# Weight tiles formed as pairs of 1024 columns in the first row, x turned tile by tile, and four smaller reorderings

## The chip, the cores and the metric

The kernel runs on one core of a Trainium2 chip. The metric is device time in microseconds (us), from the start of the program to its end; the median of three runs is given. One further execution was taken with the hardware profiler. The engines are PE (TensorE: matrix products, which end in PSUM), ACT (ScalarE), DVE (VectorE), POOL (GpSimd) and SP (which here only issues DMA transfers). Each has its own instruction stream; they wait for one another by semaphores.

## The reference

```python
# x 8x8x512x64 (B, H, S, D), state 8x8x32x64 (B, H, Ns, D)
scores = scale * x @ state^T;  xread = softmax(scores) @ state
scores2 = scale * state @ x^T; sread = softmax(scores2) @ x
x = concat([xread, sread], axis=2) -> (8 * 544, 512)
# first MoE: w_gate, w_val 512x1536, w_out 1536x512
x = (sigmoid(x @ w_gate) * (x @ w_val)) @ w_out
# second: w_in 512x1024, w_out 1024x512, g_ln 1024
h = x @ w_in
e = exp(h - max(h)); solu = h * e / (sum(e) + 1e-9)
out = ((solu - mean) / sqrt(var + 1e-6) * g_ln) @ w_out
```

x and state are float32. The weight matrices are float64, and the kernel reads each as pairs of 32-bit words.

## The kernel before

The eight batch entries are "rows" of 512 tokens. A row's first MoE runs over 12 chunks c of 128 columns of w_gate and w_val: `first_mm` forms gate and val of the chunk (gps and vps, 512 tokens each) from the attention's factors and a product state x weights, `sigma` (ACT, L658) and `gated` (DVE, L662) multiply them into sg, `gated_hi` (ACT, L134) and `gated_lo` split sg into two parts gh and gl that are multiplied apart, so that the product keeps its precision, and `out_acc` multiplies them with chunk c-1's or c's tile of w_out, itself split into woh and wol, and accumulates in acc (four banks). `mm3` issues the three partial products (L143 to L145).

In row 0 the weights come from memory as the chunks are worked on. `Conv` turns a tile of 512 float64 a partition into float32 in five steps: ACT takes the absolute high words (L207), ACT scales the low words (L208), DVE clamps (L215), shifts (L218) and puts in the sign bits (L224), POOL adds the low part (L234). A tile of w_out is then split, woh on ACT (L134) and wol on POOL (L243). `take`, `form`, `add` and `split` issue these. During chunk c, the w_out tile of c and the gate and the val tile of chunk c+2 or c+1 pass through. `banks` are two PSUM banks, att, in which ACT writes the high words and DVE works, in turn, until chunk 8; from chunk 9 on that work is done in SBUF. The last three chunks are written out behind the loop.

`state_w1(c+1)` (PE, L625) multiplies the state with the gate and val tiles of the next chunk and so needs POOL's adds of both; ACT and DVE split its result into mh (ACT, L134) and ml (DVE, L140), which `first_mm(c+1)` uses. In chunks 5 to 9 `start8` (PE, L327) forms the like product ahead for the rows that follow, in gps and vps, and ACT copies it out (est, L575); `out_acc_group` calls it between two parts of `out_acc`.

The next row's x arrives in e2t, two tiles of 512 to a group g; `a_xt_dve` transposes them on DVE (L352), and `load_xq` then loads the other group into the same buffers. The list of steps of a row is `first` and what follows it, one step for a chunk. Rows 4 to 7 read products of state and weights from the DRAM buffer qsp, by `state_load`, through a ring that `loads` fills three units ahead.

After the last row the second MoE goes tile by tile. `product` forms parts of the second product's input by a recursion that needs fewer multiplications than blocks do, `out2` multiplies by w_out (its splits woh and wol by ACT and POOL, L875), and `store` scales (L888) and writes to DRAM; a tile with `sread` tokens goes out in pieces of 32 partitions (L895), all issued by SP.

Of the kernel before, what the change touches and what calls it, by code (L numbers as in the profile page):

```python
# [28 lines left out]
def attn_moe_moe2_kernel(ctx: ExitStack, tc: tile.TileContext, x, state, w_gate, w_val, w_out, w_in2, w_out2, g_ln, out):  # L29
# [79 lines left out]
    stg0 = stg + [sbe.tile([P, 1024], F32, name=f"stge{i}") for i in range(STAGES - 2)]  # L109
# [8 lines left out]
    att = [ps.tile([P, 512], F32, name=f"att{i}") for i in range(2)]  # L118
# [3 lines left out]
    qsp = [tc.dram_tile([H, P, 512], F32, name=f"qsp{p}") for p in range(NF1 // 2)]  # L122
# [35 lines left out]
    class Conv:  # L158
# [5 lines left out]
        def __init__(self, jobs, rings):  # L164
            self.jobs = [(n, *j) for n, j in enumerate(jobs)]
            self.rings = rings
            self.pairs = 0
            self.banks, self.turns = None, 0
            self.loaded, self.taken, self.formed, self.joined, self.held = [], [], [], [], set()

        def load(self):
# [4 lines left out]
            if i in self.held:  # L176
                return
            self.jobs.pop(0)
            self.held.add(i)
# [8 lines left out]
        def take(self):  # L188
# [8 lines left out]
            else:  # L197
                t = dst
                words = s.rearrange("p (k f w) -> p k f w", k=KC, w=2)
                lo, hi = words[:, :, :, 0], words[:, :, :, 1]  # L200
            u = t
            if self.banks:
                u = self.banks[self.turns % len(self.banks)]
                self.turns += 1
                if not isinstance(dst, tuple):
                    u = u.rearrange("p (k f) -> p k f", k=KC)
            act(u, hi, AF.Abs)  # L207
            act(lo.bitcast(I32), lo.bitcast(U32), AF.Copy, scale=2.0 ** -29)  # L208
            self.taken.append((n, i, lo.bitcast(I32), hi.bitcast(U32), u, t, dst, scale))

        def bits(self, n=1):

            jobs = self.taken[:n]
            for _, _, _, _, t, _, _, _ in jobs:
                vec.tensor_scalar(out=t, in0=t, scalar1=EXP_LO, scalar2=EXP_HI, op0=ALU.max, op1=ALU.min)  # L215
            for _, _, _, _, t, _, _, _ in jobs:
                tu = t.bitcast(U32)
                vec.tensor_scalar(out=tu, in0=tu, scalar1=3, scalar2=0x3FFFFFFF, op0=ALU.logical_shift_left, op1=ALU.bitwise_and)  # L218

        def sign(self, n=1):  # L220

            jobs, self.taken = self.taken[:n], self.taken[n:]
            for n, i, lo, hi, u, t, dst, scale in jobs:
                vec.scalar_tensor_tensor(out=t.bitcast(U32), in0=hi, scalar=0xC0000000, in1=u.bitcast(U32), op0=ALU.bitwise_and, op1=ALU.bitwise_or)  # L224
                self.formed.append((i, lo, t, dst, scale))

        def form(self, n=1):
            self.bits(n)
            self.sign(n)

        def add(self):
# [3 lines left out]
            self.held.discard(i)  # L235
# [12 lines left out]
        def step(self, n):  # L248
# [6 lines left out]
            self.form(m)  # L255
# [40 lines left out]
    def load_xq(a, g):  # L296

        for q in range(2):
# [136 lines left out]
    def a_sread_mm(a, o=att[0]):  # L435
# [19 lines left out]
    def a_sread_t_mm(a=1, o=att[1]):  # L455
# [6 lines left out]
    def a_sread_t_copy(a, o=att[1]):  # L462
# [23 lines left out]
    def attention(a):  # L486
# [21 lines left out]
        def store():  # L508
# [4 lines left out]
        first = (None, lambda: a_xt_dve(a, 0))  # L513
# [48 lines left out]
    def state_load(b, n):  # L562
# [38 lines left out]
    def quad_w(pks, os):  # L601
# [7 lines left out]
        for j, ((p, k), o2) in enumerate(zip(pks, os)):  # L609
            for i, o in enumerate(o2):  # L610
# [5 lines left out]
                nc.sync.dma_start(out=qsp[p][2 * k + i], in_=s)  # L616
# [268 lines left out]
    def store(i, d=slice(0, DO), bank=None):  # L885
# [5 lines left out]
        else:  # L891
            nb = P // NS
            for e in range(nb):
                r0 = (t * nb + e) * T + S
                nc.sync.dma_start(out=out[r0:r0 + NS, d], in_=s[e * NS:(e + 1) * NS])  # L895


    def job(c, t):
        if t == 2:
            return rows(w_out, c), (woh[c], wol[c]), None  # L900
        return cols((w_gate, w_val)[t], c), wf[c // 2][:, :, c % 2, t, :], None

    def rings0(n):
        i = n % STAGES
        return (i, stg0[i]), cvt0

    def rings(n):
        return (n % 2, xn[n % 2]), tt

    jobs = [job(c, t) for c in range(2) for t in range(2)]  # L910
    for c in range(NF1):
        two = [job(c + 2, t) for t in range(2)] if c + 2 < NF1 else []
        jobs += two + [job(c, 2)] if c + 3 == NF1 else [job(c, 2)] + two
    conv = Conv(jobs, rings0)


# [66 lines left out]
    for _ in range(STAGES - 6):  # L983
# [51 lines left out]
    for _ in range(4):  # L1035
        conv.load()
    conv.banks = att
    conv.take()
    conv.take()

    def add():
        conv.add()
        conv.load()

    for c in range(NF1 - 3):
# [8 lines left out]
        add()  # L1054
        if c == 0:
            gated(c, S)
            state_w1(c + 1, acc[1])
            conv.take()
            conv.form()
            a_e2t_mm(acc[2:4])  # L1060
            a_state_first(acc[0])
        else:
            conv.take()
            if c == 1:
                a_sread_scale(acc[1], 0)
            gated(c, S)
            conv.form()
            state_w1(c + 1, gps)
        gated_hi(c, S)
# [418 lines left out]
```

## Time and profile before

| | us |
|---|---|
| three runs | 1068.93, 1068.98, 1070.4 |
| median of the runs | 1068.98 |
| the profiled execution | 1070.88 |
| its span, from first to last instruction or transfer | 1069.1 |
| PE busy in the span | 1048.3 |
| DVE, ACT, POOL busy | 746.0, 570.5, 375.9 |

The mean granted clock of PE over the span was 0.995 of full speed. Busy times of the engines overlap. A row of a timeline gives the start of an instruction, or of several alike, from the start of the span; what stands in brackets is how long the engine was idle before it and which instruction's end released it.

### The profile page before, as it was taken

The page shows a single profiled execution, that of the slowest core. Times are in us where ns is not written, and L with a number is a line of the kernel's source. Part 1 is how long each engine was busy: PE and PEld are TensorE (multiplying, and loading weights), DVE is VectorE, ACT ScalarE, POOL GpSimd, SP SyncE. Part 2 cuts the span into 40 slices and gives each one's busy share as a digit, 9 for nine tenths or more (in the row PEclk, how much of TensorE's full clock was granted, in tenths as well). Part 3 has the DMA queues.
Part 4 walks back from the last instruction along what each step waited for, and adds up shares of the span by engine and source line. Part 5 has one row for each costly group of instructions (what it writes and reads, how often), then busy time and mean ns, then how long its engine had stood idle before and what let it go on. Part 6 is the DMA issues. An engine that isn't in the chain of part 4 may idle for free.

```text
span 1069.1 us, 16670 instructions
## 1 busy us (share of the span) xinstructions
PE 1048.3 (98%) x5712; PEld 830.3 (78%) x5712; DVE 746.0 (70%) x1323; ACT 570.5 (53%) x1101; POOL 375.9 (35%) x429
## 2 busy tenths in 40 slices
PE   8889999999999999999999999999999999999998
PEld 6665666778877767878878998887888888888887
DVE  5898956667466457466464577977777787777773
ACT  5877645446335435335443355655566565655653
POOL 2687521124000000000000261345666667667551
PEclk9899999999999999999999999999999999999999
DMA  8875283461463662551531443315344444453441
GB/s 222 303 219 172 66 227 130 139 183 32 119 210 118 192 198 89 134 128 40 144 79 53 139 127 122 107 40 168 109 157 152 152 150 150 157 167 126 160 129 40
DMA packets 155741, 148.31 MB, mean 139 GB/s; under 512 B 74888, under 2 KB 115080, under 8 KB 155656
## 3 DMA queue, kind: packets, MB, share of 16 engines
q1 hardware_dynamic: 155368, 147.18, 44.9%
q8 instruction: 45, 0.74, 0.3%
q14 instruction: 40, 0.33, 0.1%
q10 hardware_dynamic: 288, 0.07, 0.0%
HBM read 91.10 MB, written 56.10 MB: 138 GB/s over the span
## 4 chain that ended last, share of the span: by engine, by line
PE 84%; DVE 6%; POOL 3%; issue 2%; DMA 2%; ACT 1%; SPq 1%; POOLq 0%; DVEq 0%; ACTq 0%
PE acc L143 11%; PE acc L145 11%; PE acc L144 11%; PE att L145 6%; PE att L143 6%; PE att L144 6%; PE gps L145 4%; PE gps L144 4%; PE gps L143 4%; PE vps L143 4%; PE vps L144 4%; PE vps L145 4%; PE gps L608 1%; POOL wf L234 1%; PE att L327 1%
## 5 line engine op out<-in xcount | busy, mean ns | idle before, releaser
L143 PE MATMUL acc<-gh,woh 128*128 128x512 f32 (+1 forms) x428 | 170.0, 397 | 0.0
L145 PE MATMUL acc<-gh,wol 128*128 128x512 f32 (+1 forms) x428 | 162.6, 380 | 0.0
L144 PE MATMUL acc<-gl,woh 128*128 128x512 f32 (+1 forms) x428 | 162.6, 380 | 0.0
L234 POOL TENSOR_TENSOR tt<-tt,xn 128x512 int32<-128x512 int32 x16 | 23.6, 1474 | 389.8 <-DVE tt L224 382.8
L662 DVE TENSOR_TENSOR sg<-vps,sg 128x512 f32<-128x512 f32 (+1 forms) x96 | 64.5, 672 | 132.4 <-PE vps L145 95.9
L658 ACT ACTIVATE sg<-gps 128x512 f32<-128x512 f32 (+1 forms) x96 | 55.9, 582 | 140.2 <-PE gps L145 137.0
L143 PEld LDWEIGHTS acc<-gh,woh 128*128 128x128 f32 x428 | 80.9, 189 | 40.3 <-issue 25.5
L134 ACT ACTIVATE gh<-sg 128x512 fp32r<-128x512 f32 (+1 forms) x102 | 61.6, 604 | 69.9 <-DVE sg L662 69.9
L145 PEld LDWEIGHTS acc<-gh,wol 128*128 128x128 f32 x428 | 80.9, 189 | 15.8
L144 PEld LDWEIGHTS acc<-gl,woh 128*128 128x128 f32 x428 | 81.0, 189 | 13.0 <-DVE gl L668 0.4
L875 POOL TENSOR_TENSOR wol<-ut,woh 128x512 fp32r<-128x512 f32 x48 | 61.6, 1298 | 79.4 <-ACT woh L134 76.7
L668 DVE TENSOR_TENSOR gl<-sg,gh 128x512 fp32r<-128x512 f32 (+1 forms) x96 | 68.1, 709 | 19.8 <-ACT gh L134 15.9
L145 PE MATMUL att<-woh,wol 128*128 128x512 f32 (+1 forms) x204 | 79.4, 389 | 0.8 <-POOL wol L875 0.8
L143 PE MATMUL att<-woh,woh 128*128 128x512 f32 (+1 forms) x204 | 79.7, 391 | 0.0
L144 PE MATMUL att<-wol,woh 128*128 128x512 f32 (+1 forms) x204 | 79.2, 388 | 0.0
L144 PE MATMUL gps<-al,mh 128*128 128x512 f32 x178 | 69.9, 393 | 1.4 <-DVE al L140 1.4
L143 PE MATMUL gps<-ah,mh 128*128 128x512 f32 x178 | 70.7, 397 | 0.3 <-ACT ah L134 0.2
L143 PE MATMUL vps<-ah,mh 128*128 128x512 f32 x178 | 69.5, 390 | 0.5 <-DVE ml L140 0.5
L145 PE MATMUL gps<-ah,ml 128*128 128x512 f32 x178 | 69.6, 391 | 0.0
L145 PE MATMUL vps<-ah,ml 128*128 128x512 f32 x178 | 69.3, 389 | 0.0
L144 PE MATMUL vps<-al,mh 128*128 128x512 f32 x178 | 69.3, 389 | 0.0
L547 POOL TENSOR_TENSOR xo<-wf,xe 128x512 fp32r<-128x512 f32 x24 | 32.3, 1354 | 97.4 <-ACT xe L134 97.4
(497 smaller groups left out, 2726.2 us busy)
## 6 DMA issues: line engine op xcount, KB each, us to landing
usp<-ub SPq DMA_DIRECT2D x32, 512.0 KB
ut<-usp SPq DMA_DIRECT2D x128, 128.0 KB
qsp<-qst SPq DMA_DIRECT2D x48, 256.0 KB
stg<-qsp SPq DMA_DIRECT2D x192, 64.0 KB
stg<-msp SPq DMA_DIRECT2D x36, 256.0 KB
out_dram<-sg SPq DMA_DIRECT2D x32, 256.0 KB
xn<-in_x_dram SPq DMA_DIRECT2D x15, 512.0 KB
msp<-pst SPq DMA_DIRECT2D x26, 256.0 KB
```

The source lines that it names most:

```text
L134: return act(dst, src, AF.Copy)
L143: mm(o, lh, rh, start=start, stop=False, **kw)
L144: mm(o, lh, rl, start=False, stop=False, **kw)
L145: return mm(o, ll, rh, start=False, stop=stop, **kw)
L234: pool.tensor_tensor(out=ti, in0=ti, in1=lo, op=ALU.add)
L327: mm(outs[e][NS * k:NS * k + NS, :], v[h, NS * k:NS * k + NS], w[k][h], start=True, stop=True)
L547: pool.tensor_tensor(out=l, in0=w, in1=r(h), op=ALU.subtract)
L608: mm(o, s[h, k, :], w[h], start=n == 0, stop=n == 2)
L658: act(sg[c % 2][:, 0:n], gate_val(b, c)[0][:, 0:n], AF.Sigmoid)
L662: vec.tensor_tensor(out=g, in0=gate_val(b, c)[1][:, 0:n], in1=g, op=ALU.mult)
L668: eng.tensor_tensor(out=gl[c % 2][:, 0:n], in0=sg[c % 2][:, 0:n], in1=r(gh[c % 2][:, 0:n]), op=ALU.subtract)
L875: pool.tensor_tensor(out=lv, in0=wv[:, 4 * q:4 * q + 4], in1=r(hv), op=ALU.subtract)
```

## The change

1. **Pairs.** In row 0 the gate and val tile of a chunk are one unit of 1024 columns, in four buffers of 2048 (before: ten of 1024, for all tiles in turn). It is loaded by two DMAs when its buffer comes free. ACT writes the high words to SBUF, where the tile will stand; the clamp goes from there to `wide`, two PSUM banks side by side; shift and sign are done from there; POOL adds 1024 columns at once. ACT's low words, the clamp, and shift and sign are now separate calls, and the clamp of the pair stands ahead of the split of the state's product (ml). `split` of the w_out tile stands behind gl, ahead of the estimate.
2. **Tenth tile.** The w_out tile that is formed in chunk 9 also passes through the bank; `att_pool` gives the banks back to att behind it.
3. **x turned tile by tile.** For the first row that takes its x this way, the two tiles of group 0 are transposed in chunks 1 and 2 (before: both in chunk 1), and half of the other group is loaded behind each.
4. **Units by one transfer.** `state_load` for rows 4 to 7 issues one DMA over 128 partitions instead of four over 32; qsp and its filling are laid out for it.
5. **Fifth product** ahead of the first `out2` and `store`.
6. **Last stores.** The last tile's pieces go out from SP and from ACT in turn.

```diff
@@ buffers
-    stg0 = stg + [sbe.tile([P, 1024], F32, name=f"stge{i}") for i in range(STAGES - 2)]
+    stg0 = [sbe.tile([P, 2048], F32, name=f"stge{i}") for i in range(STAGES // 2 - 1)]
...
-    att = [ps.tile([P, 512], F32, name=f"att{i}") for i in range(2)]
+    wide_pool = ctx.enter_context(ExitStack())
+    wide = wide_pool.enter_context(tc.tile_pool(name="psw", bufs=1, space=bass.MemoryType.PSUM)).tile([P, 1024], F32, name="wide")
+    att = [wide[:, 512 * i:512 * i + 512] for i in range(2)]
...
@@ class Conv
+            elif isinstance(src, tuple):
+                for t, part in enumerate(src):
+                    nc.sync.dma_start(out=v.rearrange("p (k t f) -> p t k f", k=KC, t=2)[:, t], in_=part)
...
-            act(u, hi, AF.Abs)
+            act(t, hi, AF.Abs)
+            self.half.append(lo)
+            self.taken.append((i, lo.bitcast(I32), hi.bitcast(U32), t, dst, scale))
+
+        def low(self):
+            lo = self.half.pop(0)
             act(lo.bitcast(I32), lo.bitcast(U32), AF.Copy, scale=2.0 ** -29)
...
+        def place(self, t):
+            if self.bank is None:
+                return t
...
+        def clamp(self):
+            t = self.taken[0][3]
+            vec.tensor_scalar(out=self.place(t), in0=t, scalar1=EXP_LO, scalar2=EXP_HI, op0=ALU.max, op1=ALU.min)
+
+        def shift(self):
+            u = self.place(self.taken[0][3]).bitcast(U32)
+            vec.tensor_scalar(out=u, in0=u, scalar1=3, scalar2=0x3FFFFFFF, op0=ALU.logical_shift_left, op1=ALU.bitwise_and)
...
+        def sign(self):
+            i, lo, hi, t, dst, scale = self.taken.pop(0)
+            vec.scalar_tensor_tensor(out=t.bitcast(U32), in0=hi, scalar=0xC0000000, in1=self.place(t).bitcast(U32), op0=ALU.bitwise_and, op1=ALU.bitwise_or)
@@ the steps of a row
+        def turned(g, q):
+            def f():
+                a_xt_dve(a, g, [q])
+                if g == 0:
+                    load_xq(a, 1, [q])
+            return f
+
+        first = [(states, None), (None, turned(0, 0)), (None, turned(0, 1))]
         return [
-            *([(states, None), first] if a == PAIR else [(states, first[1])]),
-            (None, None),
+            *(first if a == PAIR else [(states, lambda: a_xt_dve(a, 0)), (None, None)]),
@@ state_load
-        r0 = NS * (b - QUAD)
-        for k in range(KC):
-            nc.sync.dma_start(out=spill[n % 4][NS * k:NS * k + NS], in_=qsp[p][2 * k + g, r0:r0 + NS])
+        nc.sync.dma_start(out=spill[n % 4], in_=qsp[p][g].rearrange("k (n a) c -> a (k n) c", a=QUAD)[b - QUAD])
@@ store
-                nc.sync.dma_start(out=out[r0:r0 + NS, d], in_=s[e * NS:(e + 1) * NS])
+                eng = nc.scalar if i == nt - 1 and e % 2 else nc.sync
+                eng.dma_start(out=out[r0:r0 + NS, d], in_=s[e * NS:(e + 1) * NS])
@@ the units
+        if t == 3:
+            return (cols(w_gate, c), cols(w_val, c)), wf[c // 2][:, :, c % 2], None
@@ row 0, chunks 0 to 8
         conv.form()
         add()
+        conv.low()
+        if c == 1:
+            a_sread_scale(acc[1], 0)
         if c == 0:
             gated(c, S)
             state_w1(c + 1, acc[1])
-            conv.take()
-            conv.form()
+            conv.bits()
             a_e2t_mm(acc[2:4])
             a_state_first(acc[0])
         else:
-            conv.take()
-            if c == 1:
-                a_sread_scale(acc[1], 0)
             gated(c, S)
-            conv.form()
+            conv.clamp()
             state_w1(c + 1, gps)
+            conv.shift()
+        conv.sign()
         gated_hi(c, S)
         gated_lo(c, S, pool)
         if c == 0:
             a_e2t_copy(acc[2:4])
-        add()
-        conv.take()
+        conv.split()
+        conv.words()
         out_acc_group(c)
-        conv.split()
...
-        conv.form()
         add()
-        conv.take()
+        conv.low()
+        conv.words()
@@ the loop of the second MoE's tiles
         turn(i - 1)
-        if i == len(first):
-            out2(0)
-            store(0)
...
         product(i, 5, w, True, False)
         act(tmp, w, AF.Copy)
+        if i == len(first):
+            out2(0)
+            store(0)
```

On DVE, chunks 2 to 4 of row 0, this stood in the program before: sg is gated's product, att the two banks, wf the gate and val tiles, cvte the w_out tile.

```order
L662 TENSOR_TENSOR sg_110<-vps,sg_110 128x512
L215 TENSOR_SCALAR att_182<-att_182 128x512
L218 TENSOR_SCALAR att_182<-att_182 128x512
L224 SCALAR_TENSOR_TENSOR wf_145<-stge_159,att_182 128x4x128
L140 TENSOR_TENSOR ml<-gps,mh 128x2x256
L215 TENSOR_SCALAR att_183<-att_183 128x512
L218 TENSOR_SCALAR att_183<-att_183 128x512
L224 SCALAR_TENSOR_TENSOR wf_145<-stge_160,att_183 128x4x128
L215 TENSOR_SCALAR att_182<-att_182 128x512
L218 TENSOR_SCALAR att_182<-att_182 128x512
L224 SCALAR_TENSOR_TENSOR cvte_165<-stge_161,att_182 128x512
```

And this stands there now (line numbers are those of the changed kernel; L692 is gated, L232 the clamp, L147 ml, L236 the shift, L244 the sign):

```order
L692 TENSOR_TENSOR sg_110<-vps,sg_110 128x512
L232 TENSOR_SCALAR wide<-wf_145 128x1024
L147 TENSOR_TENSOR ml<-gps,mh 128x2x256
L236 TENSOR_SCALAR wide<-wide 128x1024
L244 SCALAR_TENSOR_TENSOR wf_145<-stge_158,wide 128x4x256
L232 TENSOR_SCALAR wide<-cvte_161 128x512
L236 TENSOR_SCALAR wide<-wide 128x512
L244 SCALAR_TENSOR_TENSOR cvte_161<-stg_111,wide 128x512
```

Six operations of 512 columns on the two weight tiles became three of 1024, of which one stands ahead of ml; the clamps now read SBUF and write the bank.

On POOL, chunk 5 of row 0, this stood before (gl is the low part of gated's product):

```order
L234 TENSOR_TENSOR cvte_166<-cvte_166,stge_164 128x512
L668 TENSOR_TENSOR gl_98<-sg_110,gh_96 128x512
L234 TENSOR_TENSOR wf_141<-wf_141,stg_111 128x4x128
L243 TENSOR_TENSOR wol_82<-cvte_166,woh_70 128x512
L234 TENSOR_TENSOR wf_141<-wf_141,stg_112 128x4x128
```

And this stands there now (L254 is the add, L698 gl, L263 wol):

```order
L254 TENSOR_TENSOR cvte_162<-cvte_162,stg_112 128x512
L698 TENSOR_TENSOR gl_98<-sg_110,gh_96 128x512
L263 TENSOR_TENSOR wol_82<-cvte_162,woh_70 128x512
L254 TENSOR_TENSOR wf_141<-wf_141,stge_160 128x4x256
```

wol now stands directly behind gl, and one add of 1024 columns behind it takes the place of two of 512 around it.

On PE, at the first tile of the loop of the second MoE, this is the stretch ahead of the first output (att, from woh and wol) before:

```order
L144 MATMUL acc_179<-xo_1236,ah_90 128x512
L145 MATMUL acc_179<-xe_1235,al_92 128x512
L143 MATMUL att_182<-woh_65,woh_74 128x512
L144 MATMUL att_182<-wol_77,woh_74 128x512
L145 MATMUL att_182<-woh_65,wol_86 128x512
```

And now, with the fifth product (gps, from the operands T1):

```order
L151 MATMUL acc_175<-xo_1180,ah_90 128x512
L152 MATMUL acc_175<-xe_1179,al_92 128x512
L150 MATMUL gps<-T1h_5276,gh_96 128x512
L151 MATMUL gps<-T1l_5277,gh_96 128x512
L152 MATMUL gps<-T1h_5276,gl_98 128x512
L150 MATMUL gps<-T1h_5278,gh_96 128x512
L151 MATMUL gps<-T1l_5279,gh_96 128x512
L152 MATMUL gps<-T1h_5278,gl_98 128x512
L150 MATMUL att_999<-woh_65,woh_74 128x512
```

The six matmuls of the fifth product moved from behind the first output's 24 to ahead of them.

## Rows read from the trace of the kernel before

**Rows 1.** The page's first part: busy us (share), count.
```profile
PE 1048.3 (98%) x5712; PEld 830.3 (78%) x5712; DVE 746.0 (70%) x1323; ACT 570.5 (53%) x1101; POOL 375.9 (35%) x429
```

**Rows 2.** PE's timeline, row 0: start, duration, engine, line, operation, [idle before, releaser].
```profile
39.86 0.87 PE L625 MATMUL gps<-wf,stt 128*64 128x256 f32 x6 [2.11 <-POOL wf L234]
...
63.52 0.65 PE L625 MATMUL gps<-wf,stt 128*64 128x256 f32 x4 [0.71 <-POOL wf L234]
...
71.01 1.08 PE L625 MATMUL gps<-wf,stt 128*64 128x256 f32 x8 [0.74 <-POOL wf L234]
...
74.86 0.61 PE L327 MATMUL gps<-wf,stt 64*32 64x512 f32 x1 [0.50 <-DVE ml L140]
...
80.33 0.87 PE L625 MATMUL gps<-wf,stt 128*64 128x256 f32 x6 [0.62 <-POOL wf L234]
...
106.65 0.65 PE L625 MATMUL gps<-wf,stt 128*64 128x256 f32 x4 [0.64 <-POOL wf L234]
...
116.53 0.83 PE L625 MATMUL gps<-wf,stt 128*64 128x256 f32 x5 [0.65 <-ACT sg L658]
```

**Rows 3.** DVE's timeline, chunk 3.
```profile
55.96 0.69 DVE L662 TENSOR_TENSOR sg<-vps,sg 128x512 f32<-128x512 f32 x1
56.57 0.69 DVE L215 TENSOR_SCALAR att<-att 128x512 f32<-128x512 f32 x1
...
58.02 0.69 DVE L224 SCALAR_TENSOR_TENSOR wf<-stge,att 128x512 uint32<-128x512 uint32 x1
...
63.41 0.68 DVE L662 TENSOR_TENSOR sg<-vps,sg 128x512 f32<-128x512 f32 x1
```

**Rows 4.** POOL's timeline, chunk 4.
```profile
65.88 1.30 POOL L668 TENSOR_TENSOR gl<-sg,gh 128x512 fp32r<-128x512 f32 x1 [1.00 <-ACT gh L134]
...
69.66 1.30 POOL L234 TENSOR_TENSOR wf<-wf,stge 128x512 int32<-128x512 int32 x1
```

**Rows 5.** POOL's timeline, chunk 6.
```profile
87.74 1.30 POOL L234 TENSOR_TENSOR wf<-wf,stge 128x512 int32<-128x512 int32 x1
```

**Rows 6.** Groups by line and shape, whole run: busy us, mean ns | idle before.
```profile
L716 POOL TENSOR_TENSOR gl<-e2t,gh 128x256 fp32r<-128x256 f32 x16 | 11.5, 736 | 0.0
...
L862 DVE STREAM_TRANSPOSE ub<-xn 128x1024 f32<-128x1024 f32 x22 | 27.3, 1241 | 13.0 <-ACT xn L828 13.0
```

**Rows 7.** ACT's timeline, chunk 0.
```profile
31.94 0.59 ACT L134 ACTIVATE mh<-acc 128x512 fp32r<-128x512 f32 x1
```

**Rows 8.** PE by windows: stretch, length, busy us (count), granted clock, DMA share, GB/s.
```profile
40.00:48.50 8.50, 8.46 (x34) 0.80 0.57 179
```

**Rows 9.** DVE's and PE's timelines, chunks 1 and 2 of the next row.
```profile
147.97 0.71 DVE L352 STREAM_TRANSPOSE xtr<-e2t 128x512 f32<-128x512 f32 x1 [1.91 <-DMA e2t<-in_x_dram]
150.03 0.71 DVE L352 STREAM_TRANSPOSE xtr<-e2t 128x512 f32<-128x512 f32 x1 [1.35 <-DMA e2t<-in_x_dram]
...
149.72 1.04 PE L327 MATMUL gps<-wf,stt 64*32 64x512 f32 x2
151.38 0.61 PE L327 MATMUL vps<-wf,stt 64*32 64x512 f32 x1 [0.62 <-DVE sg L662]
...
158.96 0.61 PE L327 MATMUL gps<-wf,stt 64*32 64x512 f32 x1
```

**Rows 10.** PE's timeline at the first output tile.
```profile
734.00 0.50 PE L145 MATMUL att<-woh,wol 128*128 128x512 f32 x1 [0.77 <-POOL wol L875]
```

**Rows 11.** ACT's timeline and SP's queue at the end.
```profile
1064.79 0.47 ACT L888 ACTIVATE sg<-att,stat 128x256 f32<-128x256 f32 x1 [2.27 <-PE att L145]
...
1059.89 7.10 SPq L895 DMA_DIRECT2D out_dram<-sg  x12
```

**Rows 12.** DVE's timeline, chunk 9; then a DVE group by shape.
```profile
109.39 1.16 DVE L215 TENSOR_SCALAR cvte<-cvte 128x512 f32<-128x512 f32 x1
110.59 1.42 DVE L218 TENSOR_SCALAR cvte<-cvte 128x512 uint32<-128x512 uint32 x1
...
L137 DVE CAST mh<-stg 128x512 fp32r<-128x512 f32 x6 | 2.5, 422 | 0.1
```

More of the change, by code (lines that the diff above doesn't have):

```diff
@@ L167, in __init__ @@
             self.pairs = 0
-            self.banks, self.turns = None, 0
-            self.loaded, self.taken, self.formed, self.joined, self.held = [], [], [], [], set()
+            self.bank = None
+            self.loaded, self.half, self.taken, self.formed, self.joined, self.held = [], [], [], [], [], set()
         def load(self):
@@ L186, in load, with words @@
             self.loaded.append((n, dst, scale))
-        def take(self):
+        def words(self):
             n, dst, scale = self.loaded.pop(0)
@@ L220, in sign @@
[L220 to L229, printed above, removed]
+            act(t, hi, AF.Abs)
+            self.half.append(lo)
@@ new lines, in words, with take @@
+            self.taken.append((i, lo.bitcast(I32), hi.bitcast(U32), t, dst, scale))
+        def low(self):
+            lo = self.half.pop(0)
+            act(lo.bitcast(I32), lo.bitcast(U32), AF.Copy, scale=2.0 ** -29)
+        def take(self):
+            self.words()
+            self.low()
+        def place(self, t):
+            if self.bank is None:
+                return t
+            if len(t.shape) == 3:
+                return self.bank[:, 0:KC * t.shape[2]].rearrange("p (k f) -> p k f", k=KC)
+            return self.bank[:, 0:t.shape[1]]
@@ new lines, in clamp, with bits @@
+        def clamp(self):
[4 more added lines that the diff above has]
+            vec.tensor_scalar(out=u, in0=u, scalar1=3, scalar2=0x3FFFFFFF, op0=ALU.logical_shift_left, op1=ALU.bitwise_and)
+        def bits(self):
+            self.clamp()
+            self.shift()
+        def sign(self):
+            i, lo, hi, t, dst, scale = self.taken.pop(0)
+            vec.scalar_tensor_tensor(out=t.bitcast(U32), in0=hi, scalar=0xC0000000, in1=self.place(t).bitcast(U32), op0=ALU.bitwise_and, op1=ALU.bitwise_or)
+            self.formed.append((i, lo, t, dst, scale))
@@ L231, in add, with form @@
+        def form(self):
+            self.bits()
+            self.sign()
         def add(self):
@@ L254, in step @@
                 self.take()
-            self.form(m)
+            for _ in range(m):
+                self.form()
             for _ in range(behind):
@@ L294, in xq, with load_xq @@
         return xq1[2 * g:2 * g + 2] if a == 1 else e2t
-    def load_xq(a, g):
-        for q in range(2):
+    def load_xq(a, g, qs=range(2)):
+        for q in qs:
             for j in range(4):
@@ L982, in attn_moe_moe2_kernel @@
     load_xq(1, 1)
-    for _ in range(STAGES - 6):
+    for _ in range(2):
         conv.load()
@@ L1034, in attn_moe_moe2_kernel @@
     conv.add()
-    for _ in range(4):
-        conv.load()
-    conv.banks = att
+    conv.load()
+    conv.load()
+    conv.bank = wide
     conv.take()
-    conv.take()
+    conv.words()
     def add():
         conv.add()
+        conv.load()
         conv.load()
@@ L1082, in attn_moe_moe2_kernel @@
             a_sread_t_copy(0, vps)
-        conv.form()
         add()
-        conv.take()
+        conv.low()
+        conv.words()
         if c == 0:
@@ L1097, in attn_moe_moe2_kernel @@
     first_mm(0, c, 1, 0)
-    conv.form()
-    add()
-    conv.take()
-    gated(c, S)
-    conv.form()
-    state_w1(c + 1)
+    conv.low()
+    conv.bits()
+    gated(c, S)
+    conv.sign()
+    state_w1(c + 1)
+    conv.form()
+    conv.bank = None
+    att_pool()
     gated_hi(c, S)
@@ L1119, in attn_moe_moe2_kernel @@
     sigma(c, S)
+    conv.split()
     first_mm(0, c, 1, 0)
```

70 lines of the change are left out of this document (33 added, 37 removed).

## The prediction

> **What bounds the kernel now.** I read the page's first part first: PE (TensorE) is busy 1048.3 of 1069.1 us [rows 1]. A change can then gain only where PE stands, so I went through PE's timeline for rows with idle time in front and asked each who released it. Three places matter here.
>
> In row 0 the second matrices of chunk c+1 are formed from float64 words while PE works on chunk c, and PE begins each chunk (state_w1, L625) behind POOL's last add: 2.11 us of idle before chunk 1, 0.71 and 0.74 at 63.52 and 71.01, 0.50 at 74.86 before the first estimate (start8, L327), 0.62 and 0.64 at 80.33 and 106.65, and 0.65 behind ACT at 116.53 [rows 2]. From 63.52 to 71.01 a chunk takes 7.49 us. From 80.33 to 106.65 three chunks take 26.32, 8.77 each, of which PE's own work is 8.77 - 0.63 = 8.14.
>
> Who makes POOL late differs. In chunks 2 to 4 both DVE and POOL are full: DVE goes from one gated product (L662) to the next in 63.41 - 55.96 = 7.45 with no gap [rows 3], and POOL, from gl at 65.88, starts its fourth operation at 69.66, a pitch of 1.26, and ends it 1.30 later, at 70.96 [rows 4]. From chunk 5 on it is neither: in the program woh(c) is split on ACT behind the two copies of the estimate, which end only when start8 does, so wol is late and the add behind it starts only at 87.74, 7.41 after PE's start at 80.33 [rows 2, 5], against 6.14 in chunk 4 (69.66 - 63.52).
>
> **The change in row 0.** The gate and val tiles of a chunk become one unit of 1024 columns. Two operations of 512 become one of 1024, which saves little where time goes by columns. Widths: POOL needs 736 ns for 256 columns and 1.30 us for 512 [rows 4, 6], so 0.56 per 256, and 1.30 + 1.13 = 2.4 for 1024 (two of 1.26 pitch: 2.52). DVE does 1024 columns in 1241 ns [rows 6]. For 512, gated's pitch is 0.61 (55.96 to 56.57) and clamp and shift together take 1.45 (56.57 to 58.02); the sign, of gated's form, I put at 0.61 too [rows 3]. For the pair I take clamp 1.14, shift 1.27 and sign 1.14, all near 1.24 and a little under twice the 512, since the fixed part is paid once.
>
> *DVE's chunk*: w_out tile 1.45 + 0.61 = 2.06; gated 0.61; pair 1.14 + 1.27 + 1.14 = 3.55; ml, of gated's shape, 0.61: 6.83 instead of 7.45, and 0.62 more where an x tile is transposed.
>
> *POOL's chunk* is as full as before but for one start: gl at 65.88, wol at 67.14, pair add from 68.40 to 70.80: with the 0.05 to PE, a chunk takes 7.33 instead of 7.49, -0.15. The pair's sign must be done by 68.40; DVE gives 63.41 + 0.61 + 1.14 + 0.61 + 1.27 + 1.14 = 68.18. That is 0.2 of slack, which the first rival takes up.
>
> *Chunk 0* gets worse. ACT does mh directly behind sigma, at 31.94 [rows 7]; now the 1024 low words stand between; mh takes 0.59 for 512 columns [rows 7], twice that is 1.18, and by the pipelining seen on DVE I take 1.0. mh ends at 33.5, ml at 34.2, then clamp, shift, sign 3.6 (37.9) and the add 2.4 (40.4): PE starts at 40.45, not 39.86: +0.6. Chunks 1 to 4 give back 4 x 0.15: 0 by chunk 5.
>
> *From chunk 5 on* woh and wol come before the estimate, so wol follows gl, and the last add ends 7.33 after PE's start, before PE is through its own 8.14. The wait in front of the first estimate goes with the denser DVE (-0.50), the four waits of 0.62 to 0.64 go (-2.5), and that of 0.65 at 116.53, where the tenth w_out tile was formed in SBUF with operations of 1.16 and 1.42 [rows 12], goes with the bank (-0.65). Together -3.65; with the uncertain chunks I take **-3.5**.
>
> *The unknown price* is the clamp that reads SBUF and writes PSUM beside a busy POOL: no row has it. Below: 0.42 per 512, the cast from SBUF to SBUF; above: 1.42, the slowest SBUF operation beside POOL [rows 12]. Nearest by what it writes is the clamp in the bank, 0.69 [rows 3], and I take that. At 0.42 a chunk's DVE has 0.8 more slack, which chunks 1 to 4 can't use, POOL being full. With x us more per 512, three times a chunk, row 0 comes to about -3.5 + 4 (3x - 0.5) + 4 (3x - 0.69) = 24x - 8.3, once x is over 0.23.
>
> The rows of 1.16 and 1.42 read and write SBUF, and both are slower than the same operations in the bank [rows 3, 12]. The Trainium skill, SBUF — State Buffer, § Who interferes with whom, says that a DVE instruction with at most one SBUF input, outside the modes that use two ports, does not contend with GpSimd, and its page VectorE: DVE Perf Modes, § What auto-detection actually checks, gives those modes only where source and destination are both in SBUF. By that rule the clamp stays as in the bank and row 0 gives -3.5; by the row of 1.42 (x = 0.73) it gives +9.2. The trace agrees as far as it goes (slow rows only from SBUF to SBUF), and no row has the mixed case.
>
> The clock: PE's granted clock was 0.80 in the 8.5 us from 40.0 to 48.5, between its two levels, behind stretches with idle PE [rows 8]. The change leaves gaps of 2 us there, so I leave this as it is.
>
> **x tile by tile.** In chunk 1 of the next row DVE waits for the first x tile (transposed at 147.97), then until 150.03 for the second, and gated stands behind that; PE waits for gated's result: two matmuls of the group start at 149.72, the others at 151.38; an ordinary group starts as one (158.96) [rows 9]. With the second transpose in chunk 2, gated starts 0.64 behind the first, at 148.6, before PE asks: **-1.66** (151.38 - 149.72). The reload of the second group moves with it, its first half no later than before.
>
> **Fifth product ahead.** At 734.00 PE waits 0.77 for POOL's wol of the first output [rows 10]. Six matmuls of the fifth product now stand in front; PE's mean is 1048.3 / 5712 = 0.18 each [rows 1], so they last 1.1 and cover it: **-0.77**. They read only operands made long before.
>
> **Last stores.** The last tile is ready at 1064.79 + 0.47 = 1065.26, and SP's issues end at 1066.99 [rows 11]: 1.73 for four, 0.43 each. With two on either queue the last is out 0.86 earlier; ACT has nothing after it: **-0.8**.
>
> **Unit loads of rows 4 to 7** (one DMA for four): nothing, because PE has no idle in front of what they feed: their cover is a ring filled three units ahead. If it were gone, each unit late would show as a PE wait at state_w.
>
> Sum: -3.5 - 1.66 - 0.77 - 0.8 = -6.7. The profiled execution's 1070.88 becomes 1064.2; the median of the runs is 1.9 lower (1068.98), so **1062.3**.
>
> **The rivals.**
> *A, as above*: 0.55.
> *B, the pair is late*: with a single add, nothing of chunk c+1 is ready before the whole pair is signed. If ACT's low or DVE's sign ends 1.1 later than 68.18, chunks 1 to 4 take 8.2 (+0.7 each) and chunks 5 to 8 also 8.2 (-0.57 each): 0.6 + 2.8 - 0.5 - 2.3 - 0.65 = 0 in row 0, 1065.8. For it: 0.2 of slack only. Against: ACT is half idle. 0.15.
> *C, more than I count*: the clamp runs at 0.42, or the clock stays up from 40.0 to 48.5 (8.5 x 0.2 = 1.7): 1060.6. 0.1.
> *D, the later turn moves the wait*: the second half of the reload arrives late for chunk 3 and PE waits there for some of the 1.66, 1063 to 1064; or a shallower ring of pairs makes ACT wait for a load (by the program's order a pair buffer is refilled two chunks before ACT reads it, where there were ten buffers for 24 tiles), +1 to +3 once: 1064 to 1066. 0.08.
> *E, slower*: the clamp from SBUF does contend. By 24x - 8.3, at 1.16 (x = 0.47) row 0 costs +3.0 and the whole is 1068.8, no change; at 1.42 it costs +9.2 and the time is 1074.9. It is slower from a clamp of about 1.26 per 512 on (24x = 8.3 + 3.2 + 2.1). Half of its 0.12 for each.
>
> What a measurement of this kernel can tell from no change is about 0.2%, 2.1 us: faster is below 1066.8, slower above 1071.1. A, C, and most of B and D are faster: 0.8; same 0.13 (half of E, the ends of B and D); slower 0.07. The range for 8 in 10 reaches from C's 1059.8 to the end of B and D, 1067; A's own is 1060.5 to 1064.
>
> **What would show it.** PE's state_w1 rows of row 0: pitch near 7.3 in chunks 2 to 4, 8.1 from chunk 5 on with no idle in front, and 2.7 of idle before chunk 1. DVE's clamp of 1024 columns from wf to the bank at 1.2: over 2.0 is rival E. The last POOL add of a chunk beginning right behind wol: a gap released by DVE is B. The turn's group in chunk 1 starts as one. No PE wait near 734. The end: two issues on SP and two on ACT behind the last tile. I am wrong if the pitch from chunk 5 on stays near 8.8, or a wait of the same size appears in front of the estimates or in the chunks after the turn.

## The result and the profile after

The changed kernel takes 1061.7 us (median of six runs, 1060.34 to 1064.16); over the same sessions the kernel before took 1070.54 (six runs, 1068.93 to 1072.13). The ratio is 0.992, with a 95% interval from 0.9904 to 0.9936: 6.9 to 10.3 us faster. The profiled execution takes 1061.34, its span is 1059.6 instead of 1069.1, and PE is busy 1043.8 us of it (99%).

PE's timeline in row 0, the rows that answer to [rows 2] (state_w1 is L655 now):

```profile
28.18 1.09 PE L655 MATMUL acc<-wf,stt 128*64 128x256 f32 x8 [1.98 <-POOL wf L254]
38.52 1.08 PE L655 MATMUL gps<-wf,stt 128*64 128x256 f32 x8 [2.19 <-POOL wf L254]
46.80 1.08 PE L655 MATMUL gps<-wf,stt 128*64 128x256 f32 x8
54.36 1.08 PE L655 MATMUL gps<-wf,stt 128*64 128x256 f32 x8 [0.52 <-POOL wf L254]
61.77 1.08 PE L655 MATMUL gps<-wf,stt 128*64 128x256 f32 x8 [0.65 <-POOL wf L254]
69.19 1.08 PE L655 MATMUL gps<-wf,stt 128*64 128x256 f32 x8 [0.67 <-POOL wf L254]
77.26 1.08 PE L655 MATMUL gps<-wf,stt 128*64 128x256 f32 x8
85.36 1.08 PE L655 MATMUL gps<-wf,stt 128*64 128x256 f32 x8
...
110.73 1.08 PE L655 MATMUL gps<-wf,stt 128*64 128x256 f32 x8
```

From 77.26 on nothing stands in brackets: PE no longer waits in chunks 5 to 10, and a chunk takes 85.36 - 77.26 = 8.10 instead of 8.77. Chunks 3 and 4 take 7.41 and 7.42, with a wait as before; chunk 0, 10.34, has become longer.

DVE's and POOL's timelines in chunk 4 answer to [rows 3, 4]. L232 is the clamp from SBUF to the bank, L254 the add of 1024 columns:

```profile
61.98 1.22 DVE L232 TENSOR_SCALAR wide<-wf 128x1024 f32<-128x1024 f32 x1
63.53 0.69 DVE L147 TENSOR_TENSOR ml<-gps,mh 128x512 fp32r<-128x512 f32 x1 [0.34 <-ACT mh L141]
64.14 1.22 DVE L236 TENSOR_SCALAR wide<-wide 128x1024 uint32<-128x1024 uint32 x1
65.39 1.22 DVE L244 SCALAR_TENSOR_TENSOR wf<-stge,wide 128x1024 uint32<-128x1024 uint32 x1
...
64.09 1.30 POOL L698 TENSOR_TENSOR gl<-sg,gh 128x512 fp32r<-128x512 f32 x1 [1.13 <-ACT gh L141]
65.35 1.31 POOL L263 TENSOR_TENSOR wol<-cvte,woh 128x512 fp32r<-128x512 f32 x1
66.69 2.44 POOL L254 TENSOR_TENSOR wf<-wf,stge 128x1024 int32<-128x1024 int32 x1
```

The unknown price is 1.22 for 1024 columns, the same as for the shift within the bank. The sign ends at 66.61, POOL's wol at 66.66, and POOL begins the add at 66.69.

**Where the time went.** An estimate, here and below, is a product that PE forms ahead for a later row and ACT and DVE copy out; the turn is the transposing of x. The two programs issue the same matmuls in the same order, but for the fifth product, so the start of each can be subtracted from the other. Where the difference steps, something was won or lost:

| place | step, us | forecast |
|---|---|---|
| start of chunk 0 of row 0 (28.18 for 30.06) | 1.9 | - |
| chunk 0 | -0.54 | -0.6 |
| chunks 1 to 4 | 0.48 | 0.6 |
| chunk 5 and the first estimate | 1.25 | 1.13 |
| chunks 6 to 9 | 2.73 | 2.5 |
| x tile by tile, chunk 1 | 1.66 | 1.66 |
| the chunk behind it | -0.63 | - |
| estimates in the fifth block (near 391 to 398) | 1.15 | 0 |
| fifth product | 1.05 | 0.77 |
| end, behind the last matmul | 0.68 | 0.8 |

Smaller steps of both signs make up the rest of 9.5. The first step is not the change's: `rest_only`, with row 0 as before, starts at 28.45, and `no_turn` and `late_x`, with the new row 0, at 30.16 and 30.11. The others of the table sum to 7.8. What differs at the start is how fast PE runs. Of 1.88 us, 0.74 arises at 5.65, where 16 matmuls take 1.77 us before and 1.04 after, and 1.14 where these take 1.92 before (first row) and 1.04 after:

```profile
11.90 1.92 PE L347 MATMUL vps<-ident,xn 128*64 128x128 f32 x16
```
```profile
10.52 1.04 PE L368 MATMUL vps<-ident,xn 128*64 128x128 f32 x16
```

From 10 to 14 us the mean granted clock is 0.57 of full speed before and 1.00 after. It falls between 10 and 20 us in seven of the thirteen profiled executions, and these start chunk 0 at 29.36 to 30.16; the other six start it at 27.79 to 28.52. Why it falls in some is open.

### The profile page after: what moved, and what is told of

Same layout as the page of the kernel before. It is cut to its first block, busy times and chain, and to the rows that moved or that the text cites. A ratio compares the mean times of both kernels' runs of the same rounds, so it can differ in the third digit from the quotient of the medians.

```text
span 1059.6 us, 16311 instructions
## 1 busy us (share of the span) xinstructions
PE 1043.8 (99%) x5712; PEld 828.5 (78%) x5712; DVE 732.8 (69%) x1293; ACT 567.4 (54%) x1081; POOL 375.5 (35%) x419
## 4 chain that ended last, share of the span: by engine, by line
PE 88%; DVE 5%; ACT 2%; issue 2%; DMA 2%; POOL 1%; SPq 0%; ACTq 0%; POOLq 0%; DVEq 0%
PE acc L150 12%; PE acc L152 12%; PE acc L151 12%; PE att L150 6%; PE att L152 6%; PE att L151 6%; PE gps L150 4%; PE gps L152 4%; PE vps L150 4%; PE gps L151 4%; PE vps L151 4%; PE vps L152 4%; PE gps L638 1%; PE att L348 1%; PE gps L348 1%
## 5 line engine op out<-in xcount | busy, mean ns | idle before, releaser
L692 DVE TENSOR_TENSOR sg<-vps,sg 128x512 f32<-128x512 f32 (+1 forms) x96 | 64.5, 672 | 140.3 <-PE vps L152 102.9
L254 POOL TENSOR_TENSOR tt<-tt,xn 128x512 int32<-128x512 int32 x16 | 23.6, 1473 | 385.3 <-PE att L152 337.3
L698 DVE TENSOR_TENSOR gl<-sg,gh 128x512 fp32r<-128x512 f32 (+1 forms) x96 | 64.4, 671 | 19.9 <-ACT gh L141 15.9
```

Source lines behind the costliest of these rows:

```text
L254: pool.tensor_tensor(out=ti, in0=ti, in1=lo, op=ALU.add)
L692: vec.tensor_tensor(out=g, in0=gate_val(b, c)[1][:, 0:n], in1=g, op=ALU.mult)
L698: eng.tensor_tensor(out=gl[c % 2][:, 0:n], in0=sg[c % 2][:, 0:n], in1=r(gh[c % 2][:, 0:n]), op=ALU.subtract)
```

## The experiments

For each run with a profile, this is what PE's state_w1 rows give: the start of chunk 0, and the lengths of chunks 0 to 9.

```
kernel      start   chunk 0    1    2    3    4    5    6    7    8    9
before      30.06   9.80  8.55 7.66 7.45 7.49 9.32 8.76 8.78 8.78 9.88
after       28.18  10.34  8.28 7.56 7.41 7.42 8.07 8.10 8.08 8.09 9.20
row0_only   28.47  10.33  7.64 7.41 7.42 7.41 8.07 8.09 8.09 8.10 9.21
rest_only   28.45   9.80  8.54 7.47 7.48 7.47 9.08 8.76 8.76 8.79 9.85
order_only  29.98   9.55  8.81 7.62 7.47 7.48 8.65 8.36 8.37 8.37 9.86
late_split  29.81  10.34  7.64 7.43 7.42 7.42 9.90 9.89 9.89 9.88 9.17
no_units    29.36  10.34  7.66 7.42 7.41 7.42 8.05 8.09 8.10 8.09 9.21
no_turn     30.16  10.35  8.25 7.55 7.41 7.43 8.07 8.11 8.08 8.09 9.21
low_later   28.52   9.43  7.62 7.42 7.42 7.42 8.07 8.13 8.13 8.09 9.20
gh_first    27.79  10.35  8.30 7.70 7.47 7.47 8.11 8.11 8.08 8.11 9.21
msp_act     28.50  10.32  7.65 7.43 7.41 7.42 8.09 8.09 8.09 8.13 9.20
low_msp     29.99   9.43  8.29 7.56 7.41 7.42 8.06 8.10 8.09 8.13 9.20
late_x      30.11   9.45  7.62 7.42 7.42 7.42 8.05 8.10 8.10 8.10 9.21
```

**row0_only: parts 1 and 2 alone.** The diff's hunks of the steps of a row, state_load, store and the fifth product are taken back.

> Parts 1 and 2 alone (row 0: pairs, early split, tenth tile in the bank); x turned as before, units by four DMAs, fifth product and last stores as before. Theory: row 0 gives 3.9 us between the first state_w1 and the eleventh, as in the changed kernel (offsets of PE's starts against the kernel before: about +0.5 lost in chunk 0, 0.65 to 0.7 gained in each of chunks 5 to 9), so the time is 3.5 to 4.5 us below the kernel before, some 0.996 to 0.997 of it. Rival (start-up): part of the whole gain is an earlier start of chunk 0 because the pairs are loaded differently; then PE's first state_w1 starts near 28.2 here too and the gain is 5.5 to 6 us (0.9945).

Measured: 0.9969 (0.9954 to 0.9984), 1066.75 against 1070.35. The chunks are those of the changed kernel but for chunk 1, where the clock stayed up (7.64 for 8.28), and chunks 0 to 9 take 81.77 together instead of 86.47.

**rest_only: parts 3 to 6 alone**, in the kernel before.

> Parts 3 to 6 alone (x tile by tile, units by one DMA, fifth product ahead, last stores from two queues), row 0 as before. Theory: turn 1.66 less a new wait of about 0.5, product 1.05, last stores 0.64, units 0: 2.8 to 3.3 us below the kernel before, 0.997. If the gain of 0.95 that the changed kernel shows between chunk 5 and 6 of the fifth block (PE near 391 to 397 us of the kernel before) is caused by the units by one DMA, it appears here too and the total is 3.8 to 4.3. Rival: that one is chance of a single execution: no step there. First state_w1 near 30.0 as before, if the start-up difference belongs to row 0's part.

Measured: 0.9963 (0.995 to 0.9977), 1065.89. The steps are turn 1.63 less 1.03 in the next chunk, the estimates near 391 us 0.99, product 1.04, end 0.69. By time, row 0's parts alone give 3.6 and the others alone 4.5 (each known to about 1.6), together 8.1 of the 8.8 of the whole change. Parts 2, 5 and 6 have no run of their own. For 5 and 6 the places of the steps stand in: the product's and the end's are there in all ten runs with these parts (at the end 0.66 to 0.73) and not in `row0_only` and `order_only`.

**order_only: one call moved, in the kernel before.**

```diff
         if c == 0:
             a_e2t_copy(acc[2:4])
+        conv.split()
         add()
         conv.take()
         out_acc_group(c)
-        conv.split()
```

> The kernel before with one call moved: the w_out tile is split right behind gl, ahead of the add, the next words and the estimate. Tiles stay 512 wide. Theory (the gain from chunk 5 on is one of order): POOL does gl, wol and two adds from 2.36 behind PE's start, done at 7.45, before PE's own 8.1: the four waits of 0.62 to 0.64 vanish, 2.6 to 2.8 us gained by chunk 9, the chunks 1 to 4 and the tenth tile unchanged; 0.9975. Rival (it needs the wide pairs: with 512 wide tiles DVE or POOL is still late from chunk 5 on): chunk pitch stays near 8.8, no gain.

Measured: 0.9979 (0.9966 to 0.9992), 1067.89. Chunks 6 to 8 fall from 8.77 to 8.37: POOL is in time, as the theory has it, but 8.1 is not reached, since a new wait stands in front of the estimate. PE's timeline and then DVE's:

```profile
79.56 1.08 PE L625 MATMUL gps<-wf,stt 128*64 128x256 f32 x8
...
83.14 0.61 PE L327 MATMUL gps<-wf,stt 64*32 64x512 f32 x1 [0.20 <-DVE ml L140]
```
```profile
80.34 0.69 DVE L215 TENSOR_SCALAR att<-att 128x512 f32<-128x512 f32 x1
...
82.40 0.68 DVE L140 TENSOR_TENSOR ml<-gps,mh 128x512 fp32r<-128x512 f32 x1
```

DVE does clamp, shift and sign of the first weight tile ahead of ml (80.34 to 82.40) and does not get to ml in time; in the changed kernel one clamp of 1.22 stands there. So of 0.69 a chunk, 0.41 comes with the order alone and the other 0.28 only with the pairs as well. I had given it all to the order. The pairs make DVE's operations wider and also bring ml forward, and no run tells these two apart.

**late_split: the changed kernel without that order.**

```diff
             a_e2t_copy(acc[2:4])
-        conv.split()
         conv.words()
         out_acc_group(c)
+        conv.split()
```

> The changed kernel with the split put back behind the estimate (where the kernel before has it); pairs, bank and all else as changed. Theory (order): ACT does woh behind the estimate's copies, about 5.4 behind PE's start, wol ends at 7.4, and the one add of 2.4 follows: chunks 5 to 8 take 9.8 instead of 8.1, 4 x 1.7 = 7 us more than the changed kernel, so about 2 us above to 1 below the kernel before in sum with the other parts (ratio 0.998 to 1.001). Rival (width is what gains): stays within 1 us of the changed kernel, 0.992 to 0.993.

Measured: 1.0003 (0.999 to 1.0017), 1070.4. Chunks 5 to 8 take 9.89, as expected. POOL's and PE's timelines, chunk 6:

```profile
86.11 1.32 POOL L263 TENSOR_TENSOR wol<-cvte,woh 128x512 fp32r<-128x512 f32 x1 [2.53 <-DMA stge<-in_moe_w_gate_dram]
87.38 2.42 POOL L254 TENSOR_TENSOR wf<-wf,stge 128x1024 int32<-128x1024 int32 x1
...
89.85 1.08 PE L655 MATMUL gps<-wf,stt 128*64 128x256 f32 x8 [1.75 <-POOL wf L254]
```

wol waits for woh, which ACT makes behind the estimate's copies at 85.40 (the releaser named in the first row had long been done). The whole add of 2.42 then stands behind it. Pairs without the early split would have been 1.1 a chunk worse than the kernel before.

**no_units: the changed kernel without part 4** (state_load, quad_load and qsp as before).

> The changed kernel without part 4: units of rows 4 to 7 by four DMAs again, qsp laid out as before. Theory (SP's queue): the eight issues for two units take 3.9 us of SP ahead of the loads of x and of the stores of the estimate copies, which wait for SP; the copies of the next estimate wait for those stores, and PE, near 391 to 397 us of the kernel before, loses 0.95 again: PE's offset to the kernel before stays the same there, where the changed kernel gains 0.95, and nothing else moves by over 0.3. Rival (chance of single executions): the step of 0.95 is there without the part. Time: 1.0 above the changed kernel, within what one run can't tell.

Measured in a single execution: 1061.85. The difference to the kernel before grows by only 0.3 between 180 and 730 us (times of the kernel before), where it grows by 1.2 in the changed kernel. The other runs bear this out: it grows by 0.7 (`late_x`) to 1.7 in the eight others with part 4 and by 0.1 to 0.2 in the two others without it, `row0_only` and `order_only`. About 0.9 of the 1.2 is thus the part's, and the rival is out. SP's queue of the kernel before, and then of the changed one, at the same place of the program:

```profile
380.53 3.88 SPq L569 DMA_DIRECT2D stg<-qsp  x8
384.46 4.14 SPq L302 DMA_DIRECT2D e2t<-in_x_dram  x8
388.69 1.91 SPq L616 DMA_DIRECT2D qsp<-qst  x4
```
```profile
373.70 1.05 SPq L597 DMA_DIRECT2D stg<-qsp  x2
374.80 6.05 SPq L323 DMA_DIRECT2D e2t<-in_x_dram  x8
380.94 1.90 SPq L646 DMA_DIRECT2D qsp<-qst  x4
```

Behind the unit loads stand the stores of earlier products (qsp from qst), and the next copies into qst, by ACT and DVE, wait for those stores. ACT and DVE of the kernel before, and then of the changed one:

```profile
390.90 0.60 ACT L613 ACTIVATE qst<-gps 128x512 f32<-128x512 f32 x1 [4.02 <-DMA qsp<-qst]
391.70 0.69 DVE L615 COPY qst<-vps 128x512 f32<-128x512 f32 x1 [3.28 <-DMA qsp<-qst]
394.42 1.29 DVE L352 STREAM_TRANSPOSE ee<-e2t 128x512 f32<-128x512 f32 x2
```
```profile
383.21 0.60 ACT L643 ACTIVATE qst<-gps 128x512 f32<-128x512 f32 x1 [3.17 <-PE att L638]
383.96 0.69 DVE L645 COPY qst<-vps 128x512 f32<-128x512 f32 x1 [2.38 <-DMA qsp<-qst]
386.46 1.30 DVE L373 STREAM_TRANSPOSE ee<-e2t 128x512 f32<-128x512 f32 x2
```

With the units by one transfer the stores leave 7.24 behind the first unit instead of 8.16, and ACT's copy waits for PE instead. PE gains twice. It needs the gps bank that ACT copies out: its next product there starts at 391.55 in the kernel before, as the copy ends, a loss of about 0.3. And it needs ee, which DVE transposes behind its own copies, now 12.76 behind the first unit instead of 13.89: the estimates take 1.43 us (387.36 to 388.79) instead of 2.25 (394.50 to 396.75). None of these PE rows has idle time in brackets; the loss shows only when starts are subtracted.

**no_turn: the changed kernel without part 3.**

> The changed kernel without part 3: both tiles of x transposed in chunk 1 again. Theory: the 1.66 in front of the second half of the estimates of chunk 1 is lost again, and the wait of 0.4 on ACT's estimate copy in chunk 2 is gone or below 0.2, because PE arrives later while the stores leave SP at the same time: net 1.0 to 1.3 above the changed kernel. Rival (the wait in chunk 2 comes from the earlier reload of the second group): the wait goes too and net is the 1.1 for that reason; told apart by SP's row: if the stores' issue starts as late behind the eight loads of x (some 9 to 10 us behind the copies), the reload is not what is in front of them.

Measured in a single execution: 1065.61. Of the 4.3 above the changed kernel, 2.0 is the later start and 1.4 arises behind 790 us, in waits that come in some profiles and not in others. At the end of the turn it has lost 0.7 against the changed kernel, less than the 1.0 to 1.3 expected. The stores leave SP at 146.38, 6.7 behind the copies of 139.7, and still behind eight loads of x (136.73, 7.58): the reload is not what holds them. The wait itself, in the changed kernel (pst holds the copies of the estimates, msp their place in DRAM):

```profile
144.34 2.43 SPq L615 DMA_DIRECT2D msp<-pst  x4
...
147.30 0.60 ACT L612 ACTIVATE pst<-gps 128x512 f32<-128x512 f32 x1 [4.70 <-DMA msp<-pst]
...
147.95 0.50 PE L150 MATMUL gps<-ah,mh 128*128 128x512 f32 x1 [0.38 <-ACT pst L612]
```

**low_later: chunk 0 alone.**

```diff
         add()
-        conv.low()
+        if c > 0:
+            conv.low()
...
             state_w1(c + 1, acc[1])
+            conv.low()
             conv.bits()
```

> The changed kernel, in chunk 0 alone the low words of the pair behind the state product's split (mh) instead of ahead of it. Theory: mh, ml, clamp, shift and sign come 1.0 earlier, the pair's add too, and PE's idle of 2.2 before chunk 1 falls to 1.2: 0.9 to 1.0 us below the changed kernel at that place, kept to the end. Rival (something else holds the add: the w_out tile's load or POOL): below 0.3.

Measured: 0.9921 (0.9907 to 0.9934), 1060.53. Chunk 0 takes 9.43 instead of 10.34: 0.91 less, now below the kernel before. PE's idle there did not fall (2.52, and 2.54 in `row0_only` at the same clock), since PE too gets mh earlier and finishes earlier; the start of chunk 1 moved all the same.

**gh_first: what paces chunks 1 to 4?**

```diff
             gated(c, S)
             conv.clamp()
+            gated_hi(c, S)
             state_w1(c + 1, gps)
             conv.shift()
         conv.sign()
-        gated_hi(c, S)
+        if c == 0:
+            gated_hi(c, S)
```

> The changed kernel with gh ahead of the state product's split on ACT in chunks 1 to 8, so that POOL's gl can start 1.1 earlier. Theory (DVE paces chunks 1 to 4): the pair's sign ends 4.84 behind PE's start, 0.1 ahead of POOL's add; gl and wol earlier bring at most 0.1 a chunk, 0.4 in all. Rival (the chain mh, gh, gl, wol, add on ACT and POOL paces them): chunk pitch falls from 7.41 to 6.9 or less, 2 us in all.

Measured in a single execution (1063.86): chunks 3 and 4 take 7.47, no less than before. POOL's timeline, chunk 3:

```profile
55.38 1.29 POOL L698 TENSOR_TENSOR gl<-sg,gh 128x512 fp32r<-128x512 f32 x1
56.63 1.32 POOL L263 TENSOR_TENSOR wol<-cvte,woh 128x512 fp32r<-128x512 f32 x1
59.13 2.43 POOL L254 TENSOR_TENSOR wf<-wf,stge 128x1024 int32<-128x1024 int32 x1 [1.18 <-DVE wf L244]
```

gl and wol come early, and then POOL waits 1.18 for DVE's sign. DVE and POOL are level there; relieving one gives nothing.

**msp_act and low_msp: the stores behind the turn, issued by ACT** (eng is ACT's queue in chunk 1, else SP's; `low_msp` has the edit of `low_later` too).

```diff
-            nc.sync.dma_start(out=msp[b][2 * p + g], in_=to[g])
+            eng.dma_start(out=msp[b][2 * p + g], in_=to[g])
```

> The changed kernel with the four stores of the estimates of chunk 1 of the second block issued by ACT instead of SP, where they stand behind eight loads of x that take 7.5 us of SP. Theory (SP's queue holds the stores, the stores hold the copy buffers): the stores leave at about 139 to 141 instead of 144.3 to 146.8, the copies of chunk 2 no longer wait for them, and PE's wait of 0.4 there (0.5 in the alignment of PE's starts) is gone; nothing else moves. Rival (the DMA engines themselves are full, the stores land as late whoever issues them): the wait stays at 0.3 or more.

> The changed kernel with both: the low words behind mh in chunk 0 and the stores of chunk 1 issued by ACT. If both hold, 0.9 + 0.5 = 1.4 us below the changed kernel, some 0.9905 to 0.9915 of the kernel before; if only the first, 0.992.

Measured: `msp_act` 1069.15 in a single execution, `low_msp` 0.9984 (0.9972 to 0.9996). Both theories fell short. SP, ACT and PE in `msp_act`:

```profile
134.40 8.38 SPq L323 DMA_DIRECT2D e2t<-in_x_dram  x8
...
137.38 0.60 ACT L612 ACTIVATE pst<-gps 128x512 f32<-128x512 f32 x1 [2.72 <-issue]
142.50 0.84 ACTq L615 DMA_DIRECT2D msp<-pst  x2
143.39 0.60 ACT L612 ACTIVATE pst<-att 128x512 f32<-128x512 f32 x1 [5.42 <-DMA e2t<-in_x_dram]
...
147.54 0.79 PE L150 MATMUL acc<-gh,woh 128*128 128x512 f32 x1 [5.15 <-ACT gh L141]
```

ACT's issues, too, come out only at 142.50, 4.5 behind the end of the first copy. What ACT waits for is in the trace, and it is not its turn behind SP's issues: ACT's next row names the landing of a load of x (5.42 <-DMA e2t). The program's transfers take eight semaphores in turn, each tells of one transfer's landing, and ACT waits ahead of its issue for the store's. That one was last given to the third of SP's eight loads, issued from 135.43 on, which landed at 142.43. In `low_msp` it is the same load, landed at 142.44, and ACT's issue at 142.52. On ACT the blocked issue has gh behind it: PE stood 5.15.

**late_x: the second x tile's load behind the stores, and low_later.**

```diff
-        load_xq(a, 0)
+        load_xq(a, 0, [0] if a == PAIR else range(2))
...
-                if g == 0:
-                    load_xq(a, 1, [q])
+                if q == 0:
+                    load_xq(a, 0, [1])
+                load_xq(a, 1, [q])
```

> The changed kernel with the low words behind mh in chunk 0, and the load of the second x tile of the row that is turned tile by tile issued behind the stores of the estimates of chunk 1 instead of ahead of them (the tile is needed one chunk later now). Theory (the stores are late because eight loads of x, 7.5 us, stand before them in SP's queue and in the DMA engines): the stores leave about 3 us earlier, near 141 to 143, the copies of chunk 2 and PE's wait of 0.4 to 0.5 there vanish, the tile still lands before 150; with the 0.9 of chunk 0 it is 1.4 us below the changed kernel, 0.9905 to 0.9915 of the kernel before. Rival (the DMA engines stay full and only the order changes): the second tile or the reload comes late and PE waits for it in chunk 2 or 3 by as much or more; 0.992 or above.

Measured: 0.9911 (0.9897 to 0.9924), 1060.35. The stores leave at 142.62, and no PE row from 130 to 170 has idle time in front; against `low_later` the difference steps by 0.9 there. Counted from the start of chunk 0, PE is 0.2 ahead of `low_later` at 790 us and behind it at the end, through waits late in the run; by time it can't be told from `low_later` or the changed kernel.

## Why the prediction was right, and where it was off

The forecast was 1062.3, and 1061.7 came. That is partly luck: the gain forecast, 6.7, is a little below the 6.9 to 10.3 measured, and the reference it was taken from, 1068.98, was low by 1.6, as the median of before over more runs is 1070.54. The two errors nearly cancel. By its steps:

- **Row 0, -3.5**: 3.92 in the two profiled executions. Chunk 0's loss (0.54 for 0.6), the pitch of chunks 3 and 4 (7.41 for 7.33; chunk 2 took 7.56) and the vanishing of the waits from chunk 5 on came as written. A wait of 0.62 gave back 0.69. What I had wrong is the reason in part: from chunk 5 on the order alone gives 0.41, because DVE is the next to be late (`order_only`); the rest needs the pairs, which put less ahead of ml on DVE. The order I had named as POOL's alone.
- **The clamp, 0.69 per 512**: 0.61 (1.217 for 1024 over ten instructions, 0.68 for 512). Rival E did not come. The clamp at 32.26, with POOL busy throughout (gl), takes 1.22, and so does the one at 47.58, with POOL idle. The Trainium skill, SBUF — State Buffer, § Who interferes with whom, has it so for an instruction with at most one SBUF input outside the modes that use two ports, and this trace agrees.
- **Rival B**, the pair late: its slack of 0.2 turned out as 0.05 (sign at 66.61, wol at 66.66), so DVE and POOL are level, but nothing was late beyond that.
- **The turn, -1.66**: that wait went exactly, but PE, earlier now, ran into another: at 147.95 it waits 0.38 for ACT's copy of an estimate, which waits for stores of the one before (issued 144.34, copied at 137.7). That costs 0.63. Rival D had the kind of wait right and its place and cause wrong: one chunk earlier, and not the reload but stores behind the first loads. Before, the same copy (153.43) was released by PE, which came later by the 1.66. Net 1.0; `late_x` takes the wait away.
- **Units by one transfer, 0**: about 0.9. This is the step that failed. I asked only what the loads feed (a ring three units ahead) and not what is queued behind them on SP: the stores that free the buffers of ACT's and DVE's copies. And "PE has no idle in front" was no proof: PE's ends are modelled, and this loss appears in no bracket of PE. ACT's timeline said where to look: the idle before its copy was put down to a DMA.
- **Fifth product, -0.77**: 1.05. At 726.42 the third matmul of the first output follows without a gap. The row's idle time is counted from a modelled end: the matmul ahead of that in [rows 10] starts at 732.83, so against a pitch of 0.23 PE lost 0.94, and 0.11 more in the next.
- **Last stores, -0.8**: 0.68. The queue empties 0.9 earlier in relation to the last tile, but the landing takes 2.3 instead of 2.1.
- **The clock**: I left it alone and let rival C price it at 1.7. In chunk 1 of the changed kernel it is worth 0.65: with the granted clock at 0.63 from 39 to 42 and 0.80 from 42 to 45 chunk 1 takes 8.28, and at 1.00 (`row0_only`, `low_later`, four others) 7.62 to 7.66. In the kernel before it is worth nothing there: chunk 1 takes 8.55 at the lower clock and 8.54 at full clock (`rest_only`, with 1.12 of idle in front of the next state_w1), because POOL is later anyway. With the clock up in both, chunks 0 to 9 give 4.2 (`rest_only` 86.00, `row0_only` 81.77) instead of 3.92.

The windows of the changed kernel and then of `low_later` (columns as in [rows 8]):

```profile
30.00:33.00 3.00, 2.78 (x10) 0.51 0.92 288
...
39.00:42.00 3.00, 3.00 (x12) 0.63 0.24 46
42.00:45.00 3.00, 3.00 (x12) 0.80 0.96 349
```
```profile
30.00:33.00 3.00, 2.90 (x16) 1.00 0.59 171
...
39.00:42.00 3.00, 3.00 (x15) 1.00 0.35 101
42.00:45.00 3.00, 2.69 (x12) 1.00 1.03 370
```

Both had PE idle for 2.0 us ahead of chunk 0. Why one execution falls towards 1.2 GHz behind it and the other not stays open; `late_x`, with the same row 0 as `low_later`, fell to 0.67 from 30 to 33.

## What to carry to other kernels

When a transfer is made cheaper, look at what stands behind it in the issuing queue, not only at who reads its data: the stores that free a buffer may be worth more than the load. A wait that goes uncovers the next one: ask for each engine around it how late it is itself, and take the pace from the second slowest. Two edits that are each small may need each other: the wide pairs without the early split were 1.1 a chunk slower than no change, and the early split alone gave only 0.41 of 0.69. Before a transfer is moved to another engine's queue, ask which semaphore it will wait for.

## What was unexpected

- A transfer issued by ACT is held up by a load that SP issued, through a semaphore that both use: 4.5 us (copy done at 137.98, load landed at 142.43, issue at 142.50).
- The same DVE instruction, gl in the block's chunk 2, with both inputs in SBUF, takes 0.68 in the changed kernel, where it starts at 150.21 and POOL's subtraction at 150.31 takes 1.75; in `gh_first` POOL starts first, at 150.42 with 1.29, and gl at 150.64 takes 1.61, for which PE waits 1.00. The one that starts second pays. The Trainium skill, SBUF — State Buffer, § Who interferes with whom, says that two SBUF inputs on DVE contend with a GpSimd instruction that reads SBUF, and that the order of issue decides who is held up; these rows agree.
- Single executions of one program differ by 4 us (the changed kernel's six) and up to 7 (`order_only`'s twelve). The start of chunk 0 varies from 27.8 to 30.2, with how fast PE runs in the first 20 us, and waits of 0.2 to 0.6 of PE near 800, 924, 955 and 966 us come in some profiles and not in others.
